# Gated attention plus spectral mix: first loads, first query, second block and last reciprocals rearranged

## The chip, the cores and the metric

The kernel runs on one core of a Trainium2 chip. The metric is device time in microseconds (us), the median of the runs shown. The core has a matrix engine (PE, with its weight loads shown as PEld), a vector engine (DVE), an activation engine (ACT), GpSimd (POOL) and a sync engine (SP) that mostly issues DMAs; ACT can issue DMAs too. Each engine works through its own queue of instructions in order. A wait inside a queue holds up all that is queued behind it.

## The reference

```
qkv  = x @ wqkv                      # x: 1 x 2048 x 448, 16 heads of 28
p    = softmax(q k^T * 28**-0.5)     # per head, 2048 x 2048
a    = (p @ v) heads joined @ wo
X    = rfft2(x) ; X = X * (w_r + i w_i) ; b = irfft2(X)
g    = sigmoid(sum(x * gate_w))
out  = g * a + (1 - g) * b
```

Inputs and output are bf16. The attention needs 2048 x 2048 exponentials for each of 16 heads.

## The kernel before, in words

**Tiling.** The 16 heads are four groups of four (heads in four bands of 32 partitions), the queries four chunks of 512, so there are 16 rounds, each a group and a chunk, and each round has 16 key tiles of 128. The score of a head, a key tile and a chunk is one matmul of 512 columns, a unit. The exponential of a unit is done by ACT, or, for a few key tiles of each round (the list `ND`, L547), by integer arithmetic on DVE and POOL into tiles `pd`. ACT's units are taken in steps of three and two in turn: a step's scores go into the PSUM tile `psA` (three banks) or `psB` (two banks), and one ACT instruction (L1343) takes the whole step into `ring`, which has 28 slots. There are 330 steps, numbered from 0 here. PE then multiplies each key tile's four units with the values `vw` into `pvb` (the pv matmuls, L1384); a slot of `ring` is free for a later step when its pv matmul has read it.

**Background.** Between these, PE and DVE do the projections, the transposes and the whole spectral branch through two PSUM tiles `bg`; nearly all loads and stores are issued by SP.

**Order.** A planner (`Sched.run`, L275) takes operations with an assumed duration, a key (due time) and dependences, simulates the engines, and emits the instructions in the order of the starts that it found. On the chip the instructions then stand in that order in their engine's queue, and semaphores enforce the dependences. The constants of L188 to L206 and L547 to L551 shift keys and assumed latencies. PE gaps that the planner foresees are filled with matmuls of zeros (`filler`, L953).

**Start.** `prologue` (L735) loads the small constants `cst` (ACT's queue), the first 512 rows of x in two halves (SP and ACT), and the first group's key and query weights, each in two halves (`wload`, L753): the key's on ACT's queue, the query's on SP's. PE transposes x, ACT and DVE evict the four pieces of `xT`. The weight pieces are copied into padded tiles `wpk` (by POOL, L805) and `wpq` (by DVE, L806). Then the key is projected into `psB`, the query twice: into `psA` bank 1, to be squared by ACT (L856), and into `psA` bank 0, where a matmul adds the norm row (L881). ACT and DVE evict one half each to `q` (L887, L889), and score 0 can run. `weights` (L898) issues the remaining loads on SP, the value weights `wv` and blocks 1 to 3 of x (four tiles each, L907) among them.

**First round.** `attention` (L1223) gives block b of x (512 rows, four key tiles) these steps: `x_block` (L957, transposes and evictions to `xT`; for blocks 2 and 3 one half passes through `pvb`), `proj_fast` (L1061, the key of the block: projection, scaling L1073, square L1079, norm matmul, addition L1089), `w_block` (L1095, key transposes, an ACT exponential for the key weights, L1125), `v_block` (L1145, 64 value matmuls and the scaled eviction to `vw`, L1176), and the query of chunk b (`proj_group`, L1003). Key tile 4, the first of block 1, is first used by step 6, tile 8 by step 12, tile 12 by step 19.

**End.** `normalise` (L1432) treats the last round in its own way (L1441 to L1477): ACT evicts `pvb` in two halves; four fp32 matmuls bring the sums of 128 queries each to partitions; DVE takes reciprocals and writes them, times the gate, spread over 32 columns a head, into `Rx` (a view of `Rb`); four fp32 matmuls with the identity turn them back over the partitions into `pvb` and `psA`; DVE multiplies. `last_tile` (L1540) forms the last four output tiles: the contributions of the spectral branch and of groups 0 to 2 can be added ahead, group 3's only then.

## Time and profile before

| | |
|---|---|
| median of the runs (3) | 402.31 us (401.48 to 404.51) |
| the profiled execution's own time | 401.59 us |
| its span on the core | 399.8 us |
| granted PE clock, mean | 0.998 |
| PE, ACT, DVE, POOL busy | 94%, 95%, 77%, 77% |
| first ACT exponential of a step starts at | 12.17 us |
| last one ends at | 389.94 us |

The span is what the trace shows; 1.79 us of the execution's own time lie around it. In the rows of the timeline, each has its start, its duration, engine and line, the operation with output and input tile, the shapes, how many instructions were merged, and in brackets how long the engine stood idle before and what ended that. PE matmuls are pipelined: the row of one 512-column matmul says 0.38 us, while such matmuls start every 0.21 us. Four matmuls that use 32 columns each of the array (bands of the output's partitions) run side by side, and so do up to three or four that use 32 rows each.

### The profile page before, as it was taken

What the parts mean: (1) busy time and instruction counts of PE and PEld (TensorE: products, weight loads), DVE (VectorE), ACT (ScalarE), POOL (GpSimd) and SP (SyncE); (2) the same over time, 40 slices, a digit from 0 to 9 for tenths busy, and PEclk for the clock granted to TensorE, in tenths of its full rate; (3) what the DMA queues carried; (4) which work ended last, traced back from release to release, by engine and by line L of the source; (5) the groups of instructions that cost most, each with busy time, mean ns of one, the idle gap of its engine ahead of it and who ended that gap; (6) DMA issues with size and microseconds to landing.
All of it is one profiled execution on the core that took longest, in us unless ns stands there. A gap on an engine that the chain in (4) does not pass through costs nothing.

```text
span 399.8 us, 14715 instructions
## 1 busy us (share of the span) xinstructions
PE 377.1 (94%) x6262; PEld 155.2 (39%) x6262; DVE 306.2 (77%) x579; ACT 379.8 (95%) x350; POOL 309.5 (77%) x267
## 2 busy tenths in 40 slices
PE   7989999999999999899999999999999999999996
PEld 5544433333443343324343333344333443344334
DVE  2656787988888797887888898788977767768683
ACT  3869999999999999999999999999999999999992
POOL 6027399587685968979997899899799996998840
PEclk9999999999999999999999999999999999999999
DMA  7500001211111311221122211112120322221011
GB/s 212 135 3 3 4 16 41 64 47 40 38 43 47 82 39 52 46 56 35 34 58 45 57 35 54 33 36 61 35 59 3 85 80 85 65 59 42 18 60 48
DMA packets 31191, 20.51 MB, mean 51 GB/s; under 512 B 16425, under 2 KB 29205, under 8 KB 31125
## 3 DMA queue, kind: packets, MB, share of 16 engines
q1 hardware_dynamic: 30084, 19.02, 18.1%
q8 instruction: 49, 0.80, 0.8%
q10 hardware_dynamic: 1040, 0.55, 0.5%
q14 instruction: 18, 0.14, 0.1%
HBM read 13.67 MB, written 1.97 MB: 39 GB/s over the span
## 4 chain that ended last, share of the span: by engine, by line
ACT 52%; PE 35%; issue 7%; DVE 3%; DMA 1%; ACTq 0%; POOL 0%; DVEq 0%; POOLq 0%
ACT ring L1343 51%; PE bg L689 13%; PE pvb L689 10%; PE psA L689 7%; PE psB L689 5%; DMA X<-in_A_wqkv_dram 1%; DVE vw L1176 0%; PE bg L692 0%; DVE q L1017 0%; ACTq L664 0%; DVE pd L1297 0%; DVE t L1691 0%; DVE k L1073 0%; DVE k L1017 0%; DVE sq L1027 0%
## 5 line engine op out<-in xcount | busy, mean ns | idle before, releaser
L1309 POOL TENSOR_SCALAR pd<-pd 128x2048 uint16<-128x2048 uint16 x132 | 247.7, 1898 | 39.5 <-DVE pd L1297 20.7
L1343 ACT ACTIVATE ring<-psA 128x1536 bf16<-128x1536 f32 x165 | 271.4, 1645 | 4.8 <-PE psA L689 4.8
L1343 ACT ACTIVATE ring<-psB 128x1024 bf16<-128x1024 f32 x165 | 201.3, 1220 | 0.0
L1297 DVE TENSOR_SCALAR pd<-bg 128x512 uint16<-128x512 f32 x200 | 134.2, 686 | 32.0 <-PE bg L689 28.9
L689 PEld LDWEIGHTS <-k 32*128 32x128 bf16 x1024 | 45.6, 91 | 118.6 <-issue 110.7
L689 PE MATMUL pvb<-ring,vw 128*32 128x512 bf16 x824 | 77.3, 385 | 1.7 <-DVE vw L1176 1.3
L689 PE MATMUL psA<-q,k 32*128 32x512 bf16 x495 | 64.9, 381 | 10.9 <-ACT ring L1343 7.6
L689 PE MATMUL bg<-q,k 32*128 32x512 bf16 x200 | 73.4, 382 | 0.0
L689 PE MATMUL pvb<-pd,vd 128*32 128x512 bf16 x800 | 72.0, 382 | 0.4
L689 PE MATMUL psB<-q,k 32*128 32x512 bf16 x329 | 65.7, 382 | 1.8 <-ACT ring L1343 1.2
L689 PEld LDWEIGHTS <-vw 128*32 128x32 bf16 x824 | 20.4, 94 | 34.4 <-issue 31.9
L689 PEld LDWEIGHTS <-vd 128*32 128x32 bf16 x800 | 20.9, 95 | 20.7 <-issue 16.0
L1494 POOL TENSOR_TENSOR q<-pvs,Rb 128x512 bf16<-128x512 f32 x15 | 19.1, 1273 | 7.9 <-DVE pd L1309 6.3
L689 PEld LDWEIGHTS <-xT 112*32 112x32 bf16 x1280 | 20.3, 96 | 10.8 <-issue 8.6
L1691 DVE TENSOR_TENSOR t<-bg,Wg 128x450 bf16<-128x450 f32 x32 | 19.1, 621 | 3.4 <-PE bg L689 2.2
L689 PE MATMUL pvb<-zero 128*32 128x256 bf16 (+5 forms) x416 | 19.7, 262 | 0.2 <-DVE pvs L1479 0.2
L689 PE MATMUL bg<-xT,wpq 112*32 112x512 bf16 (+1 forms) x240 | 18.2, 383 | 0.0
L689 PE MATMUL bg<-xT,wpk 112*32 112x512 bf16 (+1 forms) x240 | 17.7, 383 | 0.2 <-DVE xT L986 0.2
L689 PEld LDWEIGHTS <-zero 128*32 128x32 bf16 (+1 forms) x467 | 12.5, 97 | 12.3 <-issue 8.7
L689 PE MATMUL bg<-wo,q 128*32 128x448 bf16 x232 | 17.2, 355 | 0.0
L1129 POOL CAST vw<-w 128x16 bf16<-128x16 f32 (+1 forms) x7 | 2.3, 347 | 17.8 <-ACT w L1125 15.1
L1309 DVE TENSOR_SCALAR pd<-pd 128x2048 uint16<-128x2048 uint16 x18 | 13.9, 787 | 0.4
(131 smaller groups left out, 371.5 us busy)
## 6 DMA issues: line engine op xcount, KB each, us to landing
Rb<-rsc SPq DMA_DIRECT2D x60, 64.0 KB
CS<-cCS SPq DMA_DIRECT2D x16, 192.0 KB
xtok<-Ab SPq DMA_DIRECT2D x16, 112.5 KB
V<-xtok SPq DMA_DIRECT2D x16, 112.5 KB
xtok<-in_A_x_dram SPq DMA_DIRECT2D x3, 448.0 KB
out_dram<-fin SPq DMA_DIRECT2D x12, 112.0 KB
Wg<-in_B_w_r_dram SPq DMA_DIRECT2D x32, 28.1 KB
Wg<-in_B_w_i_dram SPq DMA_DIRECT2D x32, 28.1 KB
```

What stands on the lines that cost most here:

```text
L689: self.pin(self.nc.tensor.matmul(out, lhsT=lhsT, rhs=rhs, start=start, stop=stop, **kw))
L1129: self.pin(nc.gpsimd.tensor_copy(out=free_dims(self.vw[g][:], [[32, 16 * nb]], 4 * b0 * 128 + DH), in_=free_dims(self.w[g][:], [[1, 16 * n ...
L1297: self.pin(nc.vector.tensor_scalar(out=ys[:, s, :].bitcast(U16), in0=self.bgi(it), scalar1=127 * UNITS, scalar2=0.0, op0=ALU.add, op1=ALU. ...
L1309: self.pin(e.tensor_scalar(out=fl(pds), in0=fl(ys), scalar1=float(PHASE[f]), scalar2=1.0, op0=ALU.add, op1=ALU.mult))
L1343: self.pin(nc.scalar.activation(out=self.ring[:, u0:u0 + len(st), :], in_=slot[:, 0:len(st), :], func=ACT.Exp, scale=LN2 / UNITS))
L1494: e = self.pool(1.15, lambda: self.pin(nc.gpsimd.tensor_tensor(out=dst, in0=pvs[:], in1=self.Rb[:], op=ALU.mult)), ds, kk)
L1691: self.pin(nc.vector.tensor_tensor(out=out[:], in0=self.bgi(it)[:, 0:F2].rearrange("p (a f) -> p a f", a=2), in1=free_dims(Wg[:], [[F - 2 ...
```

## The change

- **Loads.** The first key weights go to SP's queue and the first query weights to ACT's. Block 1 of x is issued after the two loads of the value weights and no longer before them. The copies stay where they were (key by POOL, query by DVE).
- **First query.** The second projection of the first query is done in two halves of 256 columns, in banks 0 and 2 of `psA`, each with its own norm matmul and eviction.
- **Second block.** The transposes and the key projection of block 1 get keys ahead of the rest of the prologue (`X1`, `F1`); the block's transposes through `pvb` now wait for the evictions of the block before; the value and query steps of the first block get release times (`W0`, `Q1`).
- **Last reciprocals.** DVE writes one 16-column tile `rr` (reciprocal times gate); 16 fp32 matmuls of 32 output partitions each, whose stationary operand repeats one column 32 times (step zero), do the spreading.
- **Planner.** Most constants change, among them when pv matmuls are due (`PVA`, `PVD`), how long before the end the last output parts are due (`KP`), how the last round's `pd` tiles stand among its key tiles (`ELAST`), and how many of the last `pd` groups have their three phases on DVE alone (`NLD`, 2 to 3). `ND` moves a few tiles between rounds; its sum, 50, stays.

```diff
@@ -188,22 +188,25 @@
 FIRST = 0
 FWANT = (0.4, 0.45, 0.5, 0.55)
 HAND = 0.15
-XB = -1.08
+RGD = 0.25
+X1, F1 = -4975.96, -4886.98
+W0, Q1 = 6, 17.61
+XB = -0.52
 XPV = (2, 3)
 EX0, EX1 = 0.03, 0.438
 DUE_P = 6.35
-SWP = 3.47
-PVA, PVD = -2, 2.76
+SWP = 2.48
+PVA, PVD = 0.89, 3.73
 URG = 3
-FLEAD = 3.34
+FLEAD = 2.19
 SQPOOL = 0
-EL, ELAST = 2.68, 2
-NLD = 2
-KP = 60
-KN, KO, PLEAD, DSP, DHOLD, RWAIT, WREL, XLEAD, QLEAD, WLEAD = 0, 20, 1.99, 0.1, 6.53, 0.9, 27.71, 3.02, 20, 6.71
+EL, ELAST = 1.94, 5.79
+NLD = 3
+KP = 26.44
+KN, KO, PLEAD, DSP, DHOLD, RWAIT, WREL, XLEAD, QLEAD, WLEAD = 0, 7.07, 2.64, 0, 2.12, 1.74, 7.73, 4.48, 20, 5.76
 DW, DS = 0.64, 0.4
-LDMA, LREM, LRB = 2.07, 3.6, 3.2
-DUP = 1.3
+LDMA, LREM, LRB = 2.35, 2.87, 3.2
+DUP = 0.41
 
 
 def frees(o):
@@ -544,10 +547,10 @@
 
 
 class Kernel:
-    ND = [0, 4, 3, 3, 3, 2, 4, 3, 3, 4, 3, 3, 3, 4, 4, 4]
+    ND = [0, 4, 3, 3, 3, 3, 4, 3, 3, 3, 3, 3, 4, 3, 4, 4]
     RING = 28
     T0 = 10.0
-    PJE, PJV = 22.02, 21.9
+    PJE, PJV = 22.04, 21.06
     TA, TB = 37.99, 347.34
 
     def __init__(self, ctx, tc, A_x, A_wqkv, A_wo, w_r, w_i, gate_w, out):
@@ -628,7 +631,6 @@
         self.gg = T([P, 32], BF16, "gg")
         self.gT = T([32, P], BF16, "gT")
         self.G4 = T([P, 4, 16], BF16, "G4")
-        self.Rx = self.Rb[:].rearrange("p (j n) -> p j n", j=4)
         self.og = [T([P, P], BF16, f"og{i}") for i in range(4)]
         dr = ctx.enter_context(tc.tile_pool(name="drs", bufs=1, space=bass.MemoryType.DRAM))
         self.gsc = dr.tile([32, P], BF16, name="gsc")
@@ -760,8 +762,8 @@
                 r.append(self.dma(o, wsrc(off, a, n, par), deps, key + 0.1 * par, eng=eng, dur=0.6, lat=lat))
             return r
         self.wload = wload
-        dk = wload(self.wraw0["k"], D, 0, 112, K0 + 1, "AQ", lat=3.2)
-        dq = wload(self.wraw0["q"], 0, 0, 112, K0 + 2, "SP", lat=3.7)
+        dk = wload(self.wraw0["k"], D, 0, 112, K0 + 1, "SP", lat=2.9)
+        dq = wload(self.wraw0["q"], 0, 0, 112, K0 + 2, "AQ", lat=3.2)
         ms = {}
         ms["zero"] = self.pool(0.3, lambda: self.pin(nc.gpsimd.memset(self.zero[:], 0.0)), (), K0)
         ms["xt"] = self.pool(0.1, lambda: self.pin(nc.gpsimd.memset(self.xtok[:, :, D + 1:D + 2], 1.0)), (), K0 + 1)
@@ -877,17 +879,22 @@
             evs["k", lo] = self.dve(0.36, fd, (m, e), K0 + 50 + i)
             if i == 0:
                 a = square(1, self.psA[:, 1, :], 0, 512, p1q)
-                p2 = project(self.psA[:, 0, :], "q", 0, 512, K0 + 23, False)
-                m = self.pe(512, lambda: self.mm(self.psA[:, 0, :], self.c("selq"), self.sq[:, 512:1024], False, True),
-                            (a, p2), K0 + 20.5)
-                for x, eng in ((0, "ACT"), (256, "DVE")):
-                    def fe(x=x, eng=eng):
-                        o, b = self.q[0][:, x:x + 256], self.psA[:, 0, x:x + 256]
+                qb = [self.psA[:, 0, :], self.psA[:, 2, :]]
+                p2 = [project(qb[0], "q", 0, 256, K0 + 22, False), project(qb[1], "q", 256, 512, K0 + 23, False)]
+                for j, eng in ((0, "ACT"), (1, "DVE")):
+                    x = 256 * j
+
+                    def fq(j=j, x=x):
+                        self.mm(qb[j][:, x:x + 256], self.c("selq"), self.sq[:, 512 + x:768 + x], False, True)
+                    m = self.pe(256, fq, (a, p2[j]), K0 + 20.5 + .1 * j)
+
+                    def fe(j=j, x=x, eng=eng):
+                        o, b = self.q[0][:, x:x + 256], qb[j][:, x:x + 256]
                         if eng == "ACT":
                             self.pin(nc.scalar.activation(out=o, in_=b, func=ACT.Copy, scale=sv))
                         else:
                             self.pin(nc.vector.tensor_scalar(out=o, in0=b, scalar1=sv, scalar2=None, op0=ALU.mult))
-                    evs["q", x] = sc.op(eng, 0.38, fe, (m,), K0 + 49)
+                    evs["q", x] = sc.op(eng, 0.45, fe, (m,), K0 + 49)
         self.kev[0, 0] = [evs["k", 0], evs["k", 256]]
         self.qev[0, 0] = [evs["q", 0], evs["q", 256]]
         self.kfirst = evs["k", 0]
@@ -905,7 +912,7 @@
         self.wvd = {0: self.wload(self.wv0, 2 * D, 0, 112, -4988.5, "SP", lat=5.0) + gs}
         for b in range(1, 4):
             self.d_x.append(self.dma(self.xtok[:, 4 * b:4 * b + 4, 0:D], self.x[:, 4 * b:4 * b + 4, :], (self.d_x[b - 1],) if b > 1 else (),
-                                     -4990.0 + b, dur=0.45, lat=(4.0, 3.2, 5.0)[b - 1]))
+                                     -4988.0 + b, dur=0.45, lat=(3.0, 3.2, 5.0)[b - 1]))
         rw = {}
         for w, off in (("k", D), ("q", 0)):
             o = 0 if w == "q" else 4 * 336
@@ -967,7 +974,7 @@
                     def f(c=c, t=t, n=n, ci=ci, it=it, b=b):
                         o = (self.bgi(it, BF16) if it else self.pv[:].bitcast(BF16))[0:n, 512 * ci + 128 * t:512 * ci + 128 * t + 128]
                         self.tr(o, self.xtok[:, 4 * b + t, CO[c]:CO[c] + 2 * n - 1:2])
-                    ops.append(self.pe(128, f, [self.d_x[b]] + (ops[-1:] if ops or it else self.pvfree), due - 2, dur=0.07,
+                    ops.append(self.pe(128, f, [self.d_x[b]] + (ops[-1:] if ops or it else self.pvfree + [self.xev.get((b - 1, 3))]), due - 2, dur=0.07,
                                        acq=it if not ops else None))
             self.xtr.append(ops[-1])
             if half == 0:
@@ -1231,12 +1238,12 @@
         for b in range(4):
             due = ts[0] + 4 * b * rate
             if b:
-                self.x_block(b, due - XLEAD - XB * (b - 1))
-                self.proj_fast(b, due - FLEAD)
-            wop = self.w_block(0, [b], due + 5.0)
-            self.v_block(0, b, due + 6.5, wop)
+                self.x_block(b, X1 if b == 1 else due - XLEAD - XB * (b - 2))
+                self.proj_fast(b, F1 if b == 1 else due - FLEAD)
+            wop = self.w_block(0, [b], due + 5.0, W0 if b == 0 else 0.0)
+            self.v_block(0, b, due + 6.5, wop, W0 + 1.0 if b == 0 else 0.0)
         for b in range(1, 4):
-            self.proj_group("q", 0, [b], ts[b] - QLEAD, 0.0)
+            self.proj_group("q", 0, [b], ts[b] - QLEAD, Q1 if b == 1 else 0.0)
         for g in range(1, 4):
             b0 = ts[self.fr[g]] - self.PJE
             a0 = [0, 35.0, ts[4], ts[8]][g]
@@ -1455,18 +1462,18 @@
             r = self.rs[i]
             a = self.dve(0.2, lambda: self.pin(nc.vector.reciprocal(out=r[:], in_=sums[:, 0:16])), ms[-1:], kk)
             self.lastrec = a
-            xs = []
-            for h in range(2):
-                xs.append(self.dve(0.3, lambda h=h: self.pin(nc.vector.tensor_tensor(
-                    out=self.Rx[:, 2 * h:2 * h + 2, :].rearrange("p j (s n) -> p j s n", n=32),
-                    in0=free_dims(r[:], [[4, 2], [1, 4], [0, 32]], 8 * h),
-                    in1=free_dims(self.glog[:], [[1, 2], [0, 4], [0, 32]], 12 + 2 * h), op=ALU.mult)),
-                    [a, self.gate_f32, self.rblast] + xs, kk, lk=True))
+            rg = self.rr[i]
+            x = self.dve(0.1, lambda: self.pin(nc.vector.tensor_tensor(
+                out=rg[:].rearrange("p (j s) -> p j s", s=4), in0=r[:].rearrange("p (j s) -> p j s", s=4),
+                in1=free_dims(self.glog[:], [[1, 4], [0, 4]], 12), op=ALU.mult)), [a, self.gate_f32, self.nlast[i]], kk, lk=True)
             ms2 = []
             for j in range(4):
-                ms2.append(self.pe(0, lambda j=j: self.mm(home[j // 2][:, 128 * (j % 2):128 * (j % 2) + 128],
-                                                          self.Rx[:, j, :], self.c("idf").bitcast(F32), True, True),
-                                   [xs[j // 2]] + ev[1:] + ms2[-1:], kk, dur=0.25))
+                def fb(j=j):
+                    for s in range(4):
+                        self.mm(home[j // 2][32 * s:32 * s + 32, 128 * (j % 2):128 * (j % 2) + 128],
+                                free_dims(rg[:], [[0, 32]], 4 * j + s), self.c("idf").bitcast(F32), True, True,
+                                tile_position=(0, 32 * s))
+                ms2.append(self.pe(0, fb, [x] + ev[1:] + ms2[-1:], kk, mode="col", dur=RGD))
             self.onlast = []
             for j in range(2):
                 self.onlast += [self.dve(0.37, lambda j=j: self.pin(nc.vector.tensor_tensor(
```

## The prediction

> **What bounds the kernel now.** I read the page first, then ACT's waits, then the timeline of both ends, the chain of waits, and the windows. The page's slices have the engines over the span:
>
> ```profile
> PE   7989999999999999899999999999999999999996
> ACT  3869999999999999999999999999999999999992
> ```
>
> ACT is full from the fourth slice to the last but one. PE is nearly as full, but ACT sets the pace, as the list of ACT's waits (total us, times, longest) shows:
>
> ```profile
> ACT ring L1343 <- PE psA L689: 4.8, 4, 3.3
> ACT Ab L1576 <- PE bg L689: 3.9, 1, 3.9
> ```
>
> Of 330 exponentials only four waited: number 0 (0.73 us), 6 (0.19), 8 (0.61) and 12 (3.28). From number 14 (32.60) to 328 (387.79) there are 157 pairs in 355.19 us, 2.262 a pair; the shortest is 2.23. What can be had lies at the start, in the first 32 us, and after the last exponential. The timeline of the start:
>
> ```profile
> 6.14 0.42 DVE L835 COPY xT<-bg 113x512 bf16<-113x512 bf16 x1
> 6.23 0.37 POOL L789 COPY wpk<-X 112x224 bf16<-112x224 bf16 x1 [1.82 <-DMA X<-in_A_wqkv_dram]
> ...
> 7.35 0.37 POOL L792 COPY wpk<-X 112x224 bf16<-112x224 bf16 x1 [0.75 <-DMA X<-in_A_wqkv_dram]
> ...
> 9.08 0.60 ACT L856 ACTIVATE sq<-psA 128x512 bf16<-128x512 f32 x1 [0.48 <-PE psA L689]
> ...
> 11.20 0.48 DVE L889 TENSOR_SCALAR q<-psA,cst 128x256 bf16<-128x256 f32 x1 [1.30 <-ACT q L887]
> ...
> 12.17 1.45 ACT L1343 ACTIVATE ring<-psA 128x1536 bf16<-128x1536 f32 x1 [0.73 <-PE psA L689]
> ...
> 25.95 1.05 ACT L1343 ACTIVATE ring<-psB 128x1024 bf16<-128x1024 f32 x1
> 30.28 1.45 ACT L1343 ACTIVATE ring<-psA 128x1536 bf16<-128x1536 f32 x1 [3.28 <-PE psA L689]
> ```
>
> The second key half lands at 7.2, later than the last piece of x is evicted (6.56): the start waits for weights. The timeline of the end, after the last exponential (L = 389.94):
>
> ```profile
> 389.95 0.42 PE L689 MATMUL pvb<-ring,vw 128*32 128x512 bf16 x4
> 390.16 0.42 PE L689 MATMUL pvb<-pd,vd 128*32 128x512 bf16 x4
> ...
> 390.66 0.65 ACT L1445 COPY pvs<-pvb 128x256 f32<-128x256 f32 x2 [0.72 <-issue]
> ...
> 391.47 1.06 PE L689 MATMUL psA<-cst,pvs 128*128 128x4 f32 x8
> ...
> 392.98 0.76 DVE L1460 TENSOR_TENSOR Rb<-rs,glog 128x256 f32<-128x256 f32 x2
> ...
> 393.52 0.71 PE L689 MATMUL pvb<-cst,Rb 128*128 128x128 f32 x4
> ...
> 396.00 0.66 DVE L1578 TENSOR_TENSOR V<-psB,sq 128x448 bf16<-128x448 f32 x1
> ```
>
> It is a serial chain of 9.9 us.
>
> **Start to exponential 0: 0.42 us earlier.** The key's halves take the query's place on SP, and the query's take the key's on ACT's queue. Before, the key's halves were issued at 1.75 and 2.25 and landed at 6.2 and 7.2, beside the 448 KB of x block 1 that SP issued at 2.23. Now the block waits behind the two value loads and the first half of x; in the trace the second value load left at 3.9, so the block leaves at about 3.95. Without it 867 KB are ahead. By the DMA view's rates 655 KB had moved by 4.2 us; the other 212 KB, at the 148 to 277 GB/s of those small loads, end at 5.3, landing at about 5.8 (range 5.4 to 7.2, the key's time now). DVE copies the last query half before it evicts the last piece of x (queue order), so that eviction ends at 6.77 (6.56 now); the key projection then ends at 7.28, not 8.18.
>
> Half of it is given back. In PE's queue of the changed program 16 transposes of block 1 stand in this path (0.56 us each eight), so the first query half goes on at 8.9. And the program waits on `psA` as a whole: ACT's eviction of the first half waits for the third matmul of the second half, and that half's fourth waits for ACT. So 8.9 + three matmuls of 256 and the norm 0.43 + three more 0.32 + pipeline 0.17 (0.38 minus 0.21) + ACT 0.47 + two matmuls and pipeline 0.39 + DVE 0.48 + four hand-overs of 0.03 to 0.06 = 11.32 for score 0; it is 11.74 now.
>
> **From exponential 0 to 14: 1.65 us.** Block 1's key chain is done before step 6 and block 2's before step 12: its norm matmul stands ahead of score 10. So the waits at 6, 8 and 12 (4.08) go. What is late next is `ring`: steps 11 and 12 reuse the slots of key tile 0, and in the changed order the first pv matmuls stand after score 12, since `pvb` first passes blocks 2 and 3. Exactly these two exponentials wait for pv; before none did. Counted from exponential 0: number 10 at 11.35 (five pairs of 2.25, two key-weight exponentials of 0.05); score 12 after it has ended (+1.47 +0.17) at 12.99 and out at 13.3; six transposes 0.45; pipeline and ACT's key-weight exponential to 14.2; 64 value matmuls 0.95; first pv and hand-over 0.45: exponential 11 at 15.6, and not at 12.7. Number 14 follows at 18.78; now it is 32.60 - 12.17 = 20.43. If number 11 found its slot free, 2.9 us more would be gained; if PE reaches it one value block (1.0) later, 1.0 is lost.
>
> **The middle: 0.** ND's sum, the 330 steps and PE's matmuls stay. Three `pd` phases go from POOL (1.90 each) to DVE (0.69), DVE being busy 77%. Summed from the rows, PE's work between two `psA` scores exceeds 2.25 us in 37 of the pairs, 40 before, and is 4.5 us just where exponential 11 waits (4.9 at 12 before). The windows say why small stalls are all there is:
>
> ```profile
> 100.00:200.00 100.00, 96.90 (x1679) 38.49 (x1679) 83.07 (x162) 100.00 (x90) 80.05 (x60) 1.00 0.18 47
> ```
>
> Columns: stretch, sum, then busy us (instructions) of PE, PEld, DVE, ACT, POOL, then clock and DMA. In 20 pairs over 2.30 some 2 us are lost now; new places for these cost from -2 (none left) to +2 (twice as many). Nothing speaks for a sign, so 0.
>
> **The end: 0.78 us.** (1) The last pv on `pd` now precedes the last one on `ring`, and less output work stands between the last pv and the sums: 16 matmuls of groups 1 and 2 and four spectral ones, 0.87 us, after L + 0.32: sums at L + 1.20, and not L + 1.53: 0.33. (2) From reciprocal to first spreading matmul it takes 0.63 now (392.89 to 393.52). One DVE operation on 16 columns, by 0.42 for 256 and 0.28 for 128 some 0.16, with 0.21 of hand-overs: 0.37, so 0.26 less. (3) `psB`'s group 2 part moves ahead: 0.19. The spreading itself: 8 passes of 0.137 start to start (0.275 per fp32 matmul, two passes) are 1.1 us now. The 32 passes of a quarter of the columns are in no row. Bounds: 0.5 (bf16 column bands of the value matmuls start every 0.0156 us) to 4.4 (all in a row). I take 1.1, four at a time at fp32's pace, nearest in type, so no change. [...]
>
> **Sum.** 0.42 + 1.65 + 0 + 0.78 = 2.85 us. Against the profiled execution (span 399.8, its time 401.59) that is 398.74; this one ran 0.72 under the median of 402.31, and in the median's terms the result is 399.46, taken as 399.4.
>
> **Rivals.**
> - The spreading matmuls run one after another: 4.4 instead of 1.1, +3.3, so 402.8, slower than before by 0.5. All of it is on the path; it decides from 3.95 us for the 16 on. For it: no fp32 bands in the trace. Against: bf16 bands overlap. [...] Chance 0.15.
> - The last weight half lands no sooner than 7.2, since all loads share 16 DMA engines: eviction of x at 7.85, +1.1, 400.5. The same bucket holds a late x block 1: its transposes stand in PE's queue ahead of the first query, and it delays from a landing of 7.65 on; at the 4.95 us that the second key half took from issue, it would land at 9.3, +1.7, 401.1. Chance 0.17. [...]
> - The middle loses its small stalls, or exponential 11 waits less: -2 to -2.9, 397.0. For it: 37 pairs instead of 40. Chance 0.2.
> - The middle gets more stalls, +3 or more, 402.4 and up. Chance 0.08.
> - My forecast, 398.3 to 400.3: 0.4.
>
> **Numbers.** The range 396.2 to 402.6 leaves out the far ends of the last rivals, about 2 in 10. A measurement here tells some 1%, 4.0 us, from no change. Faster by over that, below 398.3: the third rival and the forecast's lower edge, 0.27. Slower, above 406.3, needs two rivals at once: 0.06. Within: 0.67.
>
> **What would show it.** Exponential 0 near 11.75; idle time of ACT before exponentials 6, 8 and 12 gone, and one of about 2.9 before number 11; number 14 near 30.5; pairs in the middle near 2.26; 9.1 us from the last exponential's end to the span's end; the spreading matmuls within 1.1 us. Wrong if ACT idles anywhere after 32 us, if the query weights are copied after 7 us, or if the spreading rows start 0.137 us apart.

## The result and the profile after

The changed kernel takes 399.24 us (median of 8 runs, 399.06 to 399.57), the kernel before 401.51 us in the same set (median of 8 runs). The ratio is 0.9934, 95% interval 0.9913 to 0.9956. The profiled execution took 399.57 us, its span is 397.75 us; before, 401.59 and 399.80.

The page's slices of the changed kernel. Both engines are as full as before, and the ends look the same at this grain:

```profile
PE   8999999999999999999999999999999999999995
ACT  3879999999999999999999999999999999999992
```

The list of ACT's waits in the changed kernel (what waited, total us, times, longest):

```profile
ACT ring L1350 <- PE pvb L691: 1.4, 1, 1.4
...
ACT w L1132 <- PE bg L694: 1.0, 1, 1.0
...
ACT ring L1350 <- PE psA L691: 0.3, 1, 0.3
```

The exponentials waited for scores in `psA` four times for 4.8 us before. Of that 0.3 is left, at exponential 0. In place of the other three stands one wait for `pvb` at number 11, and one of the key-weight exponential just ahead of it. The timeline of the changed kernel's start, to exponential 14:

```profile
5.19 0.37 POOL L791 COPY wpk<-X 112x224 bf16<-112x224 bf16 x1 [0.79 <-DMA X<-in_A_wqkv_dram]
...
5.53 0.46 PE L694 MATMUL psB<-cst,xtok 128*112 128x128 bf16 x2 [0.20 <-DMA xtok<-in_A_x_dram]
...
5.77 0.37 POOL L794 COPY wpk<-X 112x224 bf16<-112x224 bf16 x1 [0.20 <-DMA X<-in_A_wqkv_dram]
...
8.30 0.61 PE L694 MATMUL bg<-cst,xtok 128*112 128x128 bf16 x8
...
10.96 0.27 PE L691 MATMUL psA<-xT,wpq 113*128 113x256 bf16 x1 [0.56 <-ACT q L894]
...
12.48 1.45 ACT L1350 ACTIVATE ring<-psA 128x1536 bf16<-128x1536 f32 x1 [0.28 <-PE psA L691]
...
26.34 0.18 ACT L1132 ACTIVATE w<-bg 128x16 f32<-128x16 bf16 x1 [0.96 <-PE bg L694]
27.91 1.02 ACT L1350 ACTIVATE ring<-psB 128x1024 bf16<-128x1024 f32 x1 [1.38 <-PE pvb L691]
...
31.06 1.47 ACT L1350 ACTIVATE ring<-psA 128x1536 bf16<-128x1536 f32 x1
```

The key's halves are copied at 5.19 and 5.77, where POOL waited for them until 6.23 and 7.35 before. Nothing of that reaches exponential 0: it starts at 12.48, 0.31 later than before. What waits now is the second half of x (the transposes at 5.53, 5.13 before), then PE with block 1's transposes (8.30), then ACT and PE for each other (10.96). Exponential 14 follows 18.58 us after exponential 0 (20.43 before). The middle, exponentials 14 to 328, takes 355.32 us (355.19). The timeline after the last exponential, which ends at 388.53:

```profile
389.75 1.06 PE L691 MATMUL psA<-cst,pvs 128*128 128x4 f32 x8
...
390.92 0.26 DVE L1463 RECIPROCAL rs<-psA 128x16 f32<-128x16 f32 x1 [4.10 <-PE psA L691]
...
391.21 0.18 DVE L1466 TENSOR_TENSOR rr<-rs,glog 128x16 f32<-128x16 f32 x1
...
391.44 0.64 PE L691 MATMUL pvb<-cst,rr 128*32 128x128 f32 x16
...
391.90 0.62 PE L691 MATMUL psA<-cst,rr 128*32 128x128 f32 x16
...
393.87 0.65 DVE L1585 TENSOR_TENSOR V<-psB,sq 128x448 bf16<-128x448 f32 x1
```

From the last exponential's end to the span's end it is 9.22 us (9.86). The four stretches add up: +0.31 - 1.85 + 0.13 - 0.64 = -2.05, and the two spans differ by 2.05. (Numbers 328 and 329 take 2.15 us in both.)

### The profile page after: what moved, and what is told of

It reads as the page before. It is cut to its first block, busy times and chain, and to the rows that moved or that the text cites. A ratio compares the mean times of both kernels' runs of the same rounds, so it can differ in the third digit from the quotient of the medians.

```text
span 397.7 us, 14802 instructions
## 1 busy us (share of the span) xinstructions
PE 380.7 (96%) x6311; PEld 155.7 (39%) x6311; DVE 307.9 (77%) x581; ACT 379.9 (96%) x350; POOL 304.6 (77%) x264
## 4 chain that ended last, share of the span: by engine, by line
ACT 61%; PE 27%; issue 8%; DMA 1%; DVE 1%; POOL 0%; DVEq 0%; ACTq 0%; POOLq 0%
ACT ring L1350 60%; PE bg L691 10%; PE pvb L691 7%; PE psA L691 5%; PE psB L691 4%; DMA xtok<-in_A_x_dram 1%; PE bg L694 1%; DVE pd L1304 0%; POOL pd L1316 0%; ACT w L1132 0%; PE pvb L694 0%; DVE pd L1316 0%; DVE Ab L1585 0%; DVEq L1811 0%; ACT q L894 0%
## 5 line engine op out<-in xcount | busy, mean ns | idle before, releaser
L1316 POOL TENSOR_SCALAR pd<-pd 128x2048 uint16<-128x2048 uint16 x129 | 242.5, 1897 | 36.8 <-DVE pd L1304 18.5
L691 PE MATMUL pvb<-zero 128*32 128x256 bf16 (+5 forms) x432 | 18.3, 259 | 0.0
L1316 DVE TENSOR_SCALAR pd<-pd 128x2048 uint16<-128x2048 uint16 x21 | 15.0, 728 | 0.2
```

What stands on the lines that cost most here:

```text
L691: self.pin(self.nc.tensor.matmul(out, lhsT=lhsT, rhs=rhs, start=start, stop=stop, **kw))
L1316: self.pin(e.tensor_scalar(out=fl(pds), in0=fl(ys), scalar1=float(PHASE[f]), scalar2=1.0, op0=ALU.add, op1=ALU.mult))
```

## The experiments

The planner is a scheduler that places everything anew when one due time moves. So most of these kernels leave its plan alone: a function takes the finished order (a list of operations, from which each engine's queue is made) and moves a few operations in it. They are read by four stretches: exponential 0, from 0 to 14, from 14 to 328, and from the last exponential's end to the span's end.

| kernel | time, us | block 1's first transpose | exponential 0 | 0 to 14 | exponential 14 | 14 to 328 | end |
|---|---|---|---|---|---|---|---|
| before | 401.51 | 10.82 | 12.17 | 20.43 | 32.60 | 355.19 | 9.86 |
| changed | 399.24 | 8.30 | 12.48 | 18.58 | 31.06 | 355.32 | 9.22 |
| changed, again | 399.18 | 7.88 | 11.95 | 18.57 | 30.52 | 355.30 | 9.22 |
| block 1 ahead of the values | 399.86 | 9.24 | 13.41 | 18.58 | 31.99 | 355.30 | 9.21 |
| queues exchanged back | 399.26 | 8.17 | 12.24 | 18.58 | 30.82 | 355.31 | 9.22 |
| ACT's eviction later | 398.84 | 8.07 | 11.80 | 18.58 | 30.38 | 355.30 | 9.22 |
| block 1 behind the query | 399.23 | 10.48 | 11.57 | 19.19 | 30.76 | 355.30 | 9.23 |
| pv sooner | 399.32 | 8.34 | 12.42 | 18.74 | 31.16 | 355.09 | 9.23 |
| the three together | 398.81 | 9.75 | 11.10 | 19.45 | 30.55 | 355.09 | 9.21 |
| the three, mended | 398.96 | 9.65 | 11.00 | 19.40 | 30.40 | 355.29 | 9.23 |
| block 1's old due times | 405.30 | 10.18 | 11.52 | 19.40 | 30.92 | 363.75 | 9.26 |
| old planner constants | 407.10 | 8.24 | 12.31 | 18.57 | 30.88 | 359.44 | 12.95 |
| old spreading | 399.62 | 8.05 | 12.13 | 18.57 | 30.70 | 355.29 | 9.56 |
| PE in order of need | 398.23 | 7.82 | 11.55 | 17.50 | 29.05 | 355.88 | 9.20 |

The times are medians of 4 to 9 runs; the stretches are those of one profiled execution each. Two to four of these kernels at a time ran on one chip beside the kernel before, whose median was 401.36 to 401.81 there, so a few tenths of a microsecond between the times of different sets say little.

**The changed kernel again.** No edit.

> The changed kernel, unchanged, executed and profiled a second time. Theory: the 0.4 us by which the second half of x came late in its first profile (psB transposes at 5.53) belongs to that execution and not to the program: now they start at 5.0 to 5.2, the first key's square at about 7.3 and not at 7.95, block 1's transposes when block 1 lands, 8.0 to 8.4, and exponential 0 comes 4.1 us after those, at 12.1 to 12.4. Rival: the program's loads do it: 5.5 and 12.5 again. On either theory exponential 0 to 14 takes 18.58, the middle 355.3, the end 9.2.

Measured: 399.18 us. The timeline of its start:

```profile
7.88 0.66 PE L694 MATMUL bg<-cst,xtok 128*112 128x128 bf16 x8 [0.41 <-DMA xtok<-in_A_x_dram]
...
8.92 0.49 PE L691 MATMUL psA<-xT,wpq 112*128 112x256 bf16 x3
```

The second half of x is transposed at 4.82, the first key's square runs at 6.96, exponential 0 at 11.95. So the late half of x belonged to one execution: in all the other profiles of this study its transposes start between 4.82 and 5.13, and only in the first profile of the changed kernel at 5.53. What now ends last before the query goes on is block 1's landing: PE waits 0.41 us for it, then does its 16 transposes, and the second query projection starts at 8.92. In six profiles with the changed kernel's order of loads and of work at the start (one of them with the key's and the query's queues exchanged) the distance from block 1's first transpose to exponential 0 is 4.07 or 4.08 us (7.88 and 11.95, 8.05 and 12.13, 8.17 and 12.24, 8.24 and 12.31, 8.34 and 12.42) or, where the late x held the key's projection until then, 4.18 (8.30 and 12.48).

**The loads.** Block 1's transfer ahead of the two value loads, as before the change:

```
+    xb = self.d_x[1]
+    order.remove(xb)
+    order.insert(order.index(self.wvd[0][0]), xb)
```

> The changed kernel with one edit: x block 1's transfer leaves SP ahead of the two value loads, as before the change; every engine's instructions keep their order. Theory A, that the value loads (rows of 224 bytes), now running beside the second half of x, make that half late by 0.4 us: the half's first psB transposes start at about 5.1 after the span's start and not at 5.53, the last key projection ends 0.4 sooner than 7.92, and exponential 0 is at 12.1 and not at 12.48; the time falls by 0.3 to 0.4. Theory B, that it is the exchange of the key's and the query's queues: nothing changes before exponential 0 (12.5, and up to 0.4 later if block 1's 448 KB delay the key's second half). Theory C, that the landing of the second half simply varies from execution to execution by some tenths: transposes anywhere from 5.1 to 5.6, and the runs that load as the changed kernel does (the two without edit at the loads, in this set) vary as much.

Measured: 399.86 us; the second half of x is transposed at 5.13, and so it is at 5.12 or 5.13 in the three others of its set, two of which load exactly as the changed kernel does. So theory C holds and A and B fall. But exponential 0 went to 13.41. The timeline says why:

```profile
6.51 0.38 POOL L794 COPY wpk<-X 112x224 bf16<-112x224 bf16 x1 [1.76 <-DMA X<-in_A_wqkv_dram]
...
7.31 0.22 DVE L791 COPY wpq<-X 112x224 bf16<-112x224 bf16 x1 [7.31 <-DMA X<-in_A_wqkv_dram]
7.44 0.42 DVE L837 COPY xT<-pvb 112x512 bf16<-112x512 bf16 x1
```

With 448 KB of block 1 on its way, the key's second half is copied at 6.51 (5.04 to 5.77 with the changed kernel's loads) and the query's first at 7.31 (5.32 to 6.09), and DVE, which copies the query's weights ahead of its part of x, evicts that part at 7.44 instead of 5.45 to 6.24. That the weights come sooner behind the smaller loads, as the prediction had it, is shown by this; the price is block 1's own landing.

The key's weights on ACT's queue again and the query's on SP's:

```
-        dk = wload(..., K0 + 1, "SP", lat=2.9)
-        dq = wload(..., K0 + 2, "AQ", lat=3.2)
+        dk = wload(..., K0 + 1, "AQ", lat=2.9)
+        dq = wload(..., K0 + 2, "SP", lat=3.2)
```

(The planner is left to count them on the queues of the changed kernel.)

> The changed kernel with one edit: the first key weights leave on ACT's queue and the query's on SP's, as before the change; every engine's instructions keep their order. Theory A (value loads): the second half of x is late as in the changed kernel, psB transposes at 5.5. Theory B (exchange of the queues): they start at 5.1, as before the change. On either, the key's halves now come behind the second half of x on ACT's queue, so POOL copies them at about 6.1 and 6.5, where DVE copied the query's (6.09, 6.58), instead of 5.19 and 5.77; the last piece of x is evicted at 7.13, so this costs the key projection nothing or 0.1 us, and exponential 0 stays within 0.3 of 12.48. The prediction's step, that the earlier key halves are worth 0.42 us, would want 0.4 or more later.

Measured: 399.26 us, exponential 0 at 12.24 with block 1 at 8.17. The key's halves are copied at 5.52 and 5.89, the first key's square runs at 7.24. The exchange shows no gain here, 399.26 us against 399.24 and 399.18, where PE waits 0.42 us for block 1 in any case; the order of the loads behind it is what counts (block 1 ahead of the values put the key's second half at 6.51).

**The query's two halves.** ACT's eviction of the first half behind the second half's last matmul:

```
+    qe = self.qev[0, 0][0]
+    order.remove(qe)
+    order.insert(order.index(self.fq1) + 1, qe)
```

> The changed kernel with one edit: ACT's eviction of the first query half is issued behind the second half's last matmul, so that this half's fourth matmul no longer waits for ACT; each engine's own order stays. Theory: the wait of 0.56 us ahead of PE's fourth matmul (at 10.96) goes, the second half ends at about 10.5, both evictions run at about 10.7, score 0 is at 11.3 and exponential 0 at 11.8, 0.6 to 0.7 sooner; all of it is kept to exponential 14, because the wait ahead of exponential 11 moves with score 12; the time falls by 0.6. Rival: the key's projection into pvb and block 1's first key matmuls, which stand in PE's queue ahead of score 0, take the wait's place: 0.3 or less. Second rival: exponential 11's wait grows by what exponential 0 gains, and nothing is left at exponential 14.

Measured: 398.84 us (398.64 to 399.06; in the same set the exchanged queues take 399.11 to 399.45); exponential 0 at 11.80, 3.73 us after block 1's first transpose instead of 4.07. The wait of 0.56 is gone and 0.34 of it is gained, all of it kept to exponential 14. The rest went to another wait of the same kind: DVE's eviction of the second half (10.83) now waits 0.38 us for ACT's of the first, which writes the same tile `q`.

**Block 1 behind the first query.** The core of the edit (`soon`: its first eight transposes and their eviction; `late`: the other eight and the key projection; block 2's first eight go behind score 2):

```
+    for move, after in ((soon, qe), (late, sc)):
+        for o in move:
+            order.remove(o)
+        pos = max(order.index(o) for o in after) + 1
+        order[pos:pos] = move
```

> The changed kernel with block 1's work taken out of the first query's path: its first eight transposes stand behind the query's last matmul in PE's queue, its other eight and its key projection behind scores 0 and 1, block 2's first eight behind score 2; DVE's evictions move with them, and the second key half's norm goes ahead of block 1's. The loads and the two halves' wait for each other through psA stay. Theory: block 1's transposes, which wait for its landing (8.05 in the runs where the second half of x landed at 5.1) and take 0.6 for each eight, hold the second query projection until 9.1, where ACT's square of the first has long been done (8.44). Without them it starts at 8.5, and exponential 0 is at about 11.5 where it was 12.13: 0.6 sooner. Rival: block 1's own chain, now later by some 0.2 us against the clock and 0.8 against the exponentials, comes late for score 6 or holds scores 2 and 3 in PE's queue, and ACT waits again at exponentials 2, 3 or 6; then exponential 0 is sooner and exponential 14 is not (30.7).

Measured: 399.23 us. Exponential 0 is at 11.57, as the theory wanted, and exponential 14 at 30.76, as the rival did: the stretch between them grew by 0.61, pairs of 2.43 and 2.68 where the changed kernel has 2.25 and 2.30. Why is in the windows, exponential 0 to 14 of the kernel before, of the changed one and of this one (stretch, sum, then busy us of PE, PEld, DVE, ACT, POOL, clock, DMA):

```profile
12.17:32.60 20.43, 18.43 (x344) 9.55 (x344) 12.18 (x27) 16.34 (x18) 4.85 (x20) 1.00 0.16 37
```

```profile
12.48:31.06 18.58, 18.22 (x391) 9.91 (x394) 10.52 (x25) 16.24 (x17) 4.34 (x17) 1.00 0.20 47
```

```profile
11.57:30.76 19.19, 18.92 (x403) 10.21 (x406) 11.86 (x28) 16.58 (x19) 4.33 (x17) 1.00 0.24 54
```

PE was idle for 2.00 us of this stretch before, and for 0.36 and 0.27 in the other two. In the changed kernel PE is the fuller engine here, not ACT. Work moved from ahead of exponential 0 to behind it comes back as time: 0.70 us more PE work, 0.61 us more stretch.

**pv sooner.** Block 3's last transpose through `pvb` and its eviction forward, and the first two key tiles' pv ahead of the value matmuls:

```
+    order.insert(order.index(self.xg[3, 1][0]), tr)
+    order.insert(order.index(self.xev[3, 2]), ev)
+    at = max(order.index(s12), order.index(ev), order.index(wx)) + 1
+    order[at:at] = pv
```

> The changed kernel with one edit at the wait of exponential 11: the last of block 3's transposes through pvb (at 25.86, behind score 12) goes ahead of the block's transposes through the other bank, its eviction ahead of theirs on DVE, and the first two key tiles' pv matmuls go ahead of block 1's 64 value matmuls. Theory (the prediction's): exponential 11 waits for the first pv, which waits for pvb to be free of block 3 and stands behind the value matmuls; now DVE evicts pvb at 25.7 to 26.35, the first pv runs at 26.4, exponential 11 follows at 26.9 and not at 27.91: the stretch from exponential 0 to 14 falls from 18.58 to about 17.6 and the time by 1.0. Rival: score 11 or 13, or block 1's values, become late in their place, and less than 0.4 is left. Second rival: the stalls move into the middle (exponentials 14 to 328 take longer than 355.5).

(The values that stand there are block 2's and not block 1's.) Measured: 399.32 us. Exponential 11 starts at 27.16 and not at 27.91, and the gain is lost two exponentials later:

```profile
27.09 0.18 ACT L1132 ACTIVATE w<-bg 128x16 f32<-128x16 bf16 x1 [1.76 <-PE bg L694]
27.16 1.02 ACT L1350 ACTIVATE ring<-psB 128x1024 bf16<-128x1024 f32 x1
...
30.07 1.02 ACT L1350 ACTIVATE ring<-psB 128x1024 bf16<-128x1024 f32 x1 [0.54 <-PE psB L691]
```

The first pv also got ahead of block 2's last key transpose, for which the key-weight exponential waits in ACT's queue ahead of number 11 (1.76 now, 0.96 before). And score 13 still stands behind all the values and pv, whose sum is unchanged. The rival held.

**The three together**, and a second version that puts scores 2, 3 and 13 back ahead:

> The three orders together: ACT's eviction behind the query's last matmul, block 1's work behind the first query, pv ahead of the values at exponential 11. If the three waits are separate, their gains add: exponential 0 at about 11.1, exponential 0 to 14 in about 17.6, the middle and the end as in the changed kernel, 2.0 us less than its 399.2: 397.2. If block 1's chain becomes the bound, exponential 0 is at 11.1 and the stretch to 14 is longer by up to 1 us, and the time is 398.2 or more.

> The three orders of the combined kernel with PE's queue mended where it lost what they had gained: score 2 goes ahead of block 1's last two key matmuls, score 3 ahead of block 2's transposes into pvb, all four key transposes of block 1 ahead of the first two pv, and score 13 ahead of the other five pv and of block 3's key projection. Theory: in the combined kernel the 1.03 us won at exponential 0 (11.10) was lost again only because scores 2, 3 and 13 stood in PE's queue behind work that nobody was waiting for (pairs of 2.42, 2.68 and 3.09). In this order those pairs come back to 2.25, 2.30 and 2.3, exponential 11 follows pv at about 25.7, exponential 0 is at 11.1, exponential 0 to 14 takes 17.2 to 17.8, the middle stays at 355.1 to 355.4, and the time is 397.0 (2.2 under the changed kernel). Rival: what is put off (block 2's and block 3's keys, pv) is itself needed within these 20 us; then waits appear at exponentials 5 to 9 or 14 to 20, the stretch 0 to 14 or the middle is longer by over 1 us and the time is 398.3 or more.

The second version's core (`defer` puts the PE work between an operation and a score behind that score, with what depends on it):

```
+    defer(score[2], self.pg[1][2])
+    defer(score[3], [o for o in order[a + 1:] if o.eng == "PE"][0])
+    put(pv[0:2], [score[12], self.xev[3, 0]] + wx[1].deps + wx[2].deps)
+    defer(score[13], pv[2])
```

Measured: 398.81 and 398.96 us. Exponential 0 comes at 11.10 and 11.00 and exponential 14 at 30.55 and 30.40. In the second version the wait only moves on: 0.54 before exponential 4, 0.68 before number 14. Against the kernel with ACT's eviction alone (398.84; 11.80 and 30.38) 0.7 and 0.8 us are gained at exponential 0 and nothing at number 14.

**Block 1's due times of before**, the planner placing the rest anew:

```
-                self.x_block(b, X1 if b == 1 else due - XLEAD - XB * (b - 2))
-                self.proj_fast(b, F1 if b == 1 else due - FLEAD)
+                self.x_block(b, due - XLEAD - XB * (b - 1))
+                self.proj_fast(b, due - FLEAD)
```

> The changed kernel with block 1's transposes and first key projection at the due times of before; the planner then places the rest anew, so single stretches are read, not the total. Theory (the prediction's): without the early block 1 its transposes leave the first query's path (exponential 0 0.3 to 0.6 sooner than 12.13), and ACT waits again ahead of exponential 6 or 8 and of 11 or 12: exponential 0 to 14 takes 19.3 to 20.5 instead of 18.58. Rival: the gain of that stretch came from the later blocks or from what the planner does with pvb, and it stays within 0.2 of 18.58 without the early block 1.

Measured: exponential 0 at 11.52, 0 to 14 in 19.40, number 14 at 30.92. That is inside the 30.52 to 31.06 of the five profiles with the changed start and order (the changed kernel twice, the exchanged queues, the old constants, the old spreading). So, as far as a plan made anew can show it, what the early block 1 gains after exponential 0 it costs ahead of it. The waits of 0.61 and 0.19 before exponentials 8 and 6 do not come back (pairs of 2.23, 2.36, 2.53); number 11 waits 3.05. So those waits went with something else in the change, and not with block 1's early due times; what the traces say of it stands below. The total is another story: 405.30 us, with a middle of 363.75 in the profile. That profile is the longest of the four executions (407.79 us; the others took 404.97 to 405.58): ACT waits five times for 7.5 us in it, and 2.2 us of these in a stretch, 50.92 to 57.75, in which the granted PE clock is 0.50 (its mean over the profile is 0.991, in the other three executions 0.997 to 0.999).

**The planner's constants of before**, with every structural part of the change kept:

```
-SWP = 2.48
-PVA, PVD = 0.89, 3.73
+SWP = 3.47
+PVA, PVD = -2, 2.76
...
-    ND = [0, 4, 3, 3, 3, 3, 4, 3, 3, 3, 3, 3, 4, 3, 4, 4]
+    ND = [0, 4, 3, 3, 3, 2, 4, 3, 3, 4, 3, 3, 3, 4, 4, 4]
```

> The changed kernel with the planner's constants of before (lead times, penalties, the shares of the pd phases): queues, banks, block 1's early keys and the spreading stay as changed. Theory (the prediction's: the parts are worth what they are, the constants nothing): exponential 0 to 14 is 18.6, the middle stays at 355.3 within 0.5, and the end at 9.2; the time is 399.2 within 0.5. Rival: the constants are what keeps the middle at 355.3 once the early orders have moved; with the old ones it is longer by 1 us or more, as where block 1's due times alone were moved (363.75).

Measured: 407.10 us. The first 31 us are those of the changed kernel (18.57), the middle is 4.1 and the end 3.7 us longer. The rival held, at a place that nobody had named. Windows of 3 us, columns as above:

```profile
116.75:119.75 3.00, 1.56 (x16) 0.47 (x13) 3.00 (x6) 3.00 (x4) 0.00 (x0) 1.00 0.14 38
...
371.00:374.00 3.00, 2.17 (x16) 0.53 (x13) 2.59 (x5) 3.00 (x3) 2.44 (x2) 1.00 0.02 5
374.00:377.00 3.00, 2.96 (x23) 0.64 (x22) 1.18 (x3) 2.51 (x4) 3.00 (x3) 0.51 0.02 3
```

PE runs short of work for the 3 us from 371 on, and its granted clock is halved from 374 on for some 10 us (0.84 from 384 to 385, then 1.00); meanwhile ACT waits five times for 3.3 us in all, and at the end it waits 4.3 us for the last pv (0.56 in the changed kernel). The short work is not shown to be the cause: in the 3 us from 116.75 on PE has still less, and the clock stays at 1.00. The loss differs between executions: the four took 404.12 to 408.37 us, at mean clocks of 0.995 to 0.983. So what this run shows is that the constants matter for the middle and the end; through what, it leaves open.

**The old spreading** on the changed kernel: two DVE multiplications into 256 columns and eight fp32 matmuls.

```
-            x = self.dve(0.1, ... out=rg[:] ... in0=r[:] ... in1=free_dims(self.glog[:], [[1, 4], [0, 4]], 12)
+            for h in range(2):
+                xs.append(self.dve(0.3, ... out=self.Rx[:, 2 * h:2 * h + 2, :] ...
...
-                    for s in range(4):
-                        self.mm(home[j // 2][32 * s:32 * s + 32, ...], free_dims(rg[:], [[0, 32]], 4 * j + s), ...)
+                ms2.append(self.pe(0, lambda j=j: self.mm(home[j // 2][:, ...], self.Rx[:, j, :], ...
```

> The changed kernel with the last reciprocals spread as before the change: two DVE multiplications into 256 columns, then eight fp32 matmuls of 128 columns in place of 32 of a column band. Theory, from the two traces: reciprocal to first spreading matmul takes 0.89 us instead of 0.52, spreading to second product 1.20 instead of 1.15: 0.4 more, and the stretch from the last exponential's end to the span's end is 9.6 instead of 9.17; the start is that of the changed kernel (exponential 0 at 12.5). Rival: the order of the last matmuls does it, not the spreading; then the stretch stays within 0.1 of 9.17. By the prediction's terms (0.26 and nothing for the spreading) it would be 9.43.

Measured: 399.62 us, the end 9.56 us; with the new spreading and the changed kernel's constants it is 9.20 to 9.26 in eleven profiles. The theory holds, at 0.34 us against the changed kernel's 9.22; that is about half of the 0.64 by which its end is shorter than before.

**PE in order of need.** On top of ACT's later eviction, the values of block 2 (`vg[0, 2]`) go behind score 13 and block 3's key matmuls (`pg[3]`) behind score 14; `pvb` is freed of block 3 sooner, as above:

```
+    defer(score[13], [o for o in self.vg[0, 2] if order.index(o) < at])
+    defer(score[13], [o for o in self.pg[3] if order.index(o) < at])
+    at = order.index(score[14])
+    defer(score[14], [o for o in self.pg[3] if order.index(o) < at])
```

> The kernel with ACT's eviction behind the query's last matmul, and PE's queue between scores 12 and 14 put in order of need: block 3's last transpose through pvb and its eviction sooner, then the first seven key tiles' pv, score 13, and only then block 2's 64 value matmuls, score 14, and block 3's 16 key matmuls. PE does the same work. Theory: PE's queue is full in this stretch (busy 18.2 of the 18.58 us from exponential 0 to 14), so what counts is what stands ahead of scores 13 and 14 in it: 1.85 us of values and keys are put off, pv runs at about 25.6, exponential 11 starts at 26.0 (27.2 in the kernel with ACT's eviction alone), number 14 at 29.3 and not at 30.38, and the later pairs, which have 0.1 to 0.5 us of PE to spare each, take up the work: 397.8. Rival: no such room: what is put off makes exponentials 15 to 25 wait, and the time stays at 398.6 to 399.0.

Measured: 398.23 us (398.09 to 398.56), beside 399.18 (398.80 to 399.54) for the changed kernel on the same chip; against the kernel before the ratio is 0.9911, 95% interval 0.9891 to 0.9932. The timeline of ACT:

```profile
25.90 1.02 ACT L1350 ACTIVATE ring<-psB 128x1024 bf16<-128x1024 f32 x1 [0.36 <-PE pvb L691]
...
29.05 1.47 ACT L1350 ACTIVATE ring<-psA 128x1536 bf16<-128x1536 f32 x1
30.76 1.02 ACT L1350 ACTIVATE ring<-psB 128x1024 bf16<-128x1024 f32 x1 [0.24 <-PE psB L691]
```

Numbers 11 and 14 start at 25.90 and 29.05 (26.0 and 29.3 expected), and 0 to 14 takes 17.50, as expected; the rest of the lead is an early block 1 (7.82), which put exponential 0 at 11.55 and not at 11.80. Part of it is paid back: number 15 waits 0.24, and the middle is 0.58 longer. This is the fastest kernel of the study.

## Why the prediction was right, and where not

**The total.** 399.4 was forecast and 399.24 measured, but that it came so near is luck: two errors cancel in it. Against the profiled execution the working gave 398.74, and that one took 399.57. And the step from the profiled execution to the median, +0.72, rested on the three runs with a median of 402.31; the median of eight is 401.51, and the profiled 401.59 stood at it, not under it.

**Start to exponential 0: 0.42 earlier. This step failed**: 0.31 later in the first profile, 0.22 earlier in the second, between these in four others of the same start (against one profile of before, 12.17). Its first half was right: weights and projection came as worked out (the key's projection at 7.28; the square that follows it starts at 6.89 to 7.44 in the profiles with the changed kernel's loads, but for the first, 7.95). Its second half was not. It let the 16 transposes of block 1 run as soon as PE was free, so that "the first query half goes on at 8.9". But block 1, issued at 3.77 to 3.91 where about 3.95 was forecast, landed between 7.82 and 8.34 in seven profiles, and PE, in whose queue the transposes stand ahead of the query, waited 0.25 to 0.54 us for it. The prediction had named this as a part of its second rival, a delay "from a landing of 7.65 on", and put a chance on it instead of a term in the sum: 11.75 and the 0.2 to 0.7 beyond 7.65 are 12.0 to 12.4, where exponential 0 is found. In the first profile the late half of x comes to the same. The chain through `psA`, the whole-tile wait included, ran in the forecast's order, but from the first half's going on to score 0 it took 2.59 us in the second profile (8.92 to 11.51) and not 2.42: the four hand-overs, taken as 0.03 to 0.06 each, are 0.32 together and not 0.16. That the sum beyond 7.65 comes out all the same is chance, since the transposes and the norm ahead of it took 1.04 where it had left 1.25. What the whole-tile wait costs as an order is 0.34 (ACT's eviction later).

**Exponential 0 to 14: 1.65.** Measured 1.85, number 11 at 15.43 after number 0 (15.6). The waits at 6, 8 and 12 went and the new one came where the prediction said, behind the first pv; of the idle time, about 2.9 forecast, 2.34 was found, 0.96 before the key-weight exponential and 1.38 before number 11. But two of its reasons are thinner than they read. The waits at 6 and 8 stay away without the early block 1 too. The trace of the kernel before shows what stood ahead of scores 6 (18.89) and 8 (21.86) in PE's queue, value matmuls and the first pv, and that each waited for DVE:

```profile
18.67 0.29 PE L689 MATMUL bg<-wv,xT 112*32 112x113 bf16 x8 [0.29 <-DVE q L1017]
...
21.31 0.61 PE L689 MATMUL pvb<-ring,vw 128*32 128x512 bf16 x8 [0.73 <-DVE vw L1176]
```

Block 1's keys were added at 18.53 and 21.08, behind the same two DVE operations, the scaling of chunk 1's query (17.86) and of block 0's values (20.55). In the changed kernel PE projects that query behind score 7 and not ahead of score 5, and the first pv stands behind score 12; with block 1's old due times they stand behind scores 9 and 12. So the late query (its release time is `Q1`) and the late pv are the likely cause. This is read from the orders: no run moves either alone, and none takes the release times or the query's two halves out of the change. And the 2.9 us "more" if number 11 found its slot free were not to be had by freeing the slot: with pv sooner, score 13 became late in its place. PE's queue was the limit in this stretch, 18.22 us of 18.58.

**The middle: 0.** Measured +0.13, 19 pairs over 2.30 (20 before). Right for this kernel, but the bound of 2 us on either side was too narrow for what stands behind it: in the profile with the old constants the same structure loses 4.1 us there, in the one with block 1's old due times 8.4, both with a stretch of halved clock.

**The end: 0.78.** Measured 0.64. Sums 0.31 sooner (0.33); reciprocal's end to first spreading matmul 0.26 instead of 0.63, so 0.37 (0.26); group 2 in `psB` nothing: from the second product to the last addition it is 1.28 us in both (0.19 forecast). Of these only the spreading was tested by a run of its own. Sixteen spreading passes start within 0.46 us, 391.44 to 391.90, so 32 take about 0.92, and 1.1 was assumed. The first rival, passes one after another at 0.137 us, did not come: the trace shows 0.029 us a pass (0.46 for the 16).

## What to carry to other kernels

When a step is moved forward in an engine's queue, its operand's landing is a term of the sum and not a rival: work out when it lands, and who stands behind it in the queue (here PE waited 0.25 to 0.54 us for block 1, with the first query behind it). Before pricing a wait, read which engine is full in that stretch alone: where the matrix engine is busy 98% of it, as here, a wait taken away came back at the next score or two, and what gained was to put work off past the stretch. Tuned constants of a planner belong to the arrangement they were tuned for; a structural edit is to be judged by stretches, and its constants are a part of it. Where the granted clock changed inside a stretch, as in two of these profiles (0.50 for 10.2 and 6.8 us), its length can't be put down to the edit alone.

## What the runs showed of the hardware

In the profile with the old constants the granted TensorE clock went from 1.00 to 0.50 at 374.08 us, after a window of 3 us with PE busy for 2.17 us and no idle gap over 0.64 us. It stayed there for 10.2 us, in which PE was busy for 2.96, 3.00 and 3.00 us of the 3 us from 374, 377 and 380 on. In the profile with block 1's old due times it was 0.50 from 50.92 to 57.75 us. A thin window did not bring it everywhere: in the old constants' own trace PE is busy for 1.56 of the 3 us from 116.75 on, and the clock stays at 1.00. What brought the two falls stays open.

Landings varied between executions by some tenths of a microsecond: block 1 from 7.82 to 8.34 in kernels that issue it alike (3.77 to 3.91), the second half of x 0.4 us late in one profile of fourteen (transposed at 5.53, and at 4.82 to 5.13 in the others). A difference of that size at the start, read from one pair of traces, is not an effect of the edit until a second profile shows it.
